# Cosformer attention with a mixture of adapters: v issued earlier, the adapter transpose copied by VectorE, and a new order in a few places

## The chip, the cores and the metric

The kernel runs on one core of one Trainium2 chip. The metric is the device time of one execution in microseconds (us); lower is better. Five engines work side by side, each through its own queue in program order: TensorE (PE in the profile, its weight loads PEld), VectorE (DVE), ScalarE (ACT), GpSimd (POOL) and SyncE (SP), which here only issues transfers. Transfers (DMAs) are issued from SP, from POOL and, at the very end, from ACT.

## What is computed

Two steps, cut to what matters. Inputs q, k, v are 8 batches x 8 heads x 576 positions x 64 floats; the output is 4608 x 512 floats.

```
phi(x) = concat(relu(x) * cos_w, relu(x) * sin_w)      # per position, 64 -> 128 features
kv  = einsum('bhsf,bhsd->bhfd', phi(k), v)             # 128 x 64 per batch and head
z   = sum over s of phi(k)
num = phi(q) @ kv ;  den = phi(q) @ z + 1e-6
x   = (num / den), heads side by side: 4608 rows x 512

logits = x @ w_gate                                    # 8 adapters
topk = the two largest; w = softmax over the two
out = x + sum over the two of w * ((x @ A[e]) @ B[e])  # rank 16 adapters
```

## The kernel before

**Tiles and slots.** The 4608 rows are 36 tiles of 128 rows (NT = 36). A tile has two "columns" of 64 rows (a batch and a residue of its positions modulo 9), so 9 tiles make a pair of batches. The main loop (L433) has one step per tile, called slot n below. A slot holds the work of several tiles in different stages: tile n is normalised, the numerators and denominators of tile n+1 are computed, the scaled q of tile n+2 is transposed, q of tile n+3 is scaled. The order is written out by hand: the helpers are called in the order in which each engine shall get its instructions, and the tiles' semaphores make an engine wait at the head of its queue until the operands are there.

**Attention.** `scale_k(u)` makes phi(k) of one of 72 units (batch b, residue i; u = 9b + i) with two ScalarE instructions (L159, L170). `kv(u)` (L187) adds 8 small matmuls into the PSUM tile `kvz`; after the ninth unit of a batch `kv_out` (L192) copies it to SBUF. The table `kv_at` says in which slot which units are multiplied; their `scale_k` stands one slot ahead. `scale_q` (L205) makes phi(q) without the relu on GpSimd, `transp_q` (L215) transposes it on TensorE, `evac_q` (L220) applies the relu and copies it out on VectorE, `numden` (L229, L234) multiplies with kv, and `normalise` (L241, L243) divides.

**Adapters.** `transp_x` (L250) and `evac_x` (L255) bring x of tile n to the other layout in the PSUM tile `xz` (columns 0 to 511), `logits` (L276) multiplies by A and w_gate. Tiles form groups of three (the last two groups have two and one). For a group whose last tile is t, slot t+1 ("age 1") has `gate_max` (three small VectorE operations and two on GpSimd, nm L296 and tg L298). Slot t+2 ("age 2") has the sigmoid `gate_sig` (L306, ScalarE), the masking `gate_em` (L313, GpSimd), `gate_b` (L340, VectorE) and `transp_z` (L348), which transposes zg into columns 512 to 895 of the same `xz`. Slot t+3 ("age 3") begins with `evac_z` (L356), which copies this to `zgT` on ScalarE. From there on one `delta` per slot adds x (L366) and the adapters' share (L367) in the single PSUM tile `dx`; `evac_o` (L375, ScalarE) copies it out and `store` (L387) issues two transfers from SP. Ages 1, 2 and 3 follow each other, so every slot from 3 on is one of the three kinds; the age 3 slots are 5, 8, 11 and so on to 32, and tile 35 is handled behind the loop.

**Loads.** k and q come as fp32 from SP (1152 KB per batch; four buffers each, the first v sharing those of k). v of batches 1 to 7 is cast to bf16 by transfers that GpSimd issues (L83; four buffers); v of batch 0 comes as fp32 and is cast on the engines (L413 to L416). The tables at L400 and L401 say at the end of which slot a load is called: k and q of batches 4 to 7 in slots 1, 5, 10 and 14, v of batches 2 to 7 in slots 3, 6, 9, 13, 17 and 21. v of batch 1 is called before the loop (L421), behind the scaling of tile 0. A load stands in its issuing engine's queue like any other instruction: an SP load is behind the stores called before it, a GpSimd load is behind the `scale_q` and gate operations called before it.

**Buffers that matter.** `qp` has 3, `kp` 10, `osb` (what is stored) 14; `xz`, `dx`, `kvz`, `nd` and the transposed q have one PSUM tile each.

**The end.** Behind the loop (L486 to L522) tile 35 and the last six deltas are written out one by one; the za, nd and dx tiles serve as accumulators there.

Of the kernel before, what the change touches and what calls it, by code (L numbers as in the profile page):

```python
# [25 lines left out]
def kernel(ctx, tc, q, k, v, w_gate, A, Bw, out):  # L26
    nc = tc.nc
# [53 lines left out]
    def load_v(b):  # L81
        t = v_bufs[b % NV][:, 0:VL].rearrange("p (j x) -> p j x", j=HP)
        nc.gpsimd.dma_start(out=t, in_=part(v, b))  # L83
# [113 lines left out]
        cols = [(2 * m, i) for i in range(NC)] + [(2 * m + 1, i) for i in range(NC)]  # L197
        return cols[2 * s:2 * s + 2]

    def scale_q(n, x, eng=None):  # L200
        if x == 0:
            qp_t[n] = p_qp.tile([128, 2, HP, 2, D], BF16, name="qp")
        b, i = columns(n)[x]
        for t, tab in ((0, cos_tab), (1, sin_tab)):
            (eng or nc.gpsimd).tensor_scalar(out=qp_t[n][:, x, :, t, :], in0=q_t[b][:, :, i, :],  # L205
                                             scalar1=tab[:, i:i + 1], scalar2=1.0,
                                             op0=ALU.mult, op1=ALU.mult)

# [14 lines left out]
    def numden(n):  # L223
        nd_t[n] = nd = ps.tile([128, 2, 512], FP32, name="nd")
        qpT = qpT_t.pop(n)
        (b0, _), (b1, _) = columns(n)
        jobs = [(slice(0, 128), b0)] if b0 == b1 else [(lo, b0), (hi, b1)]
        for gg in range(2):
            nc.tensor.matmul(out=nd[:, gg, D:4 * W:W], lhsT=ones, rhs=eps_hi, start=True,  # L229
                             stop=False, skip_group_check=True)  # L230
            for jj in range(4):
                h = gg * 4 + jj
                for pr, b in jobs:
                    nc.tensor.matmul(out=nd[pr, gg, jj * W:(jj + 1) * W], lhsT=qpT[:, h, pr],  # L234
                                     rhs=kv_t[b][:, h % 2, h // 2, :],
                                     start=False, stop=(jj == 3), skip_group_check=True)
# [13 lines left out]
            nc.tensor.transpose(out=xz[:, c * 128:(c + 1) * 128],  # L250
                                in_=xt_t[n][:, c:DM:DCH], identity=ident)

    def evac_x(n):
        xT_t[n] = t = p_xt.tile([128, DCH, 128], BF16, name="xT")
        nc.vector.tensor_copy(t, xz[:, 0:512].rearrange("p (c s) -> p c s", c=DCH))  # L255

    groups = [list(range(i, min(i + 3, NT - 3))) for i in range(0, NT - 3, 3)]
    groups += [[NT - 3, NT - 2], [NT - 1]]
# [89 lines left out]
            nc.tensor.transpose(out=xz[:, 512 + i * 128:512 + (i + 1) * 128], in_=zg[:, i],  # L348
                                identity=ident)

    def evac_z(g, on_act=False):
        G = len(groups[g])
        zgT_t[g] = t = p_g.tile([128, 3, 128], BF16, name="zgT")
        src = xz[:, 512:512 + G * 128].rearrange("p (c s) -> p c s", c=G)
        if on_act:
            nc.scalar.copy(t[:, 0:G], src)  # L356
        else:
            nc.vector.tensor_copy(t[:, 0:G], src)

    def delta(n, bank=None):  # L360
        g = group_of[n]
        if bank is None:
            dx = ps.tile([128, DM], FP32, name="dx", tag="dx")
        else:
            dx = bank
        nc.tensor.matmul(out=dx, lhsT=ident, rhs=xt_t.pop(n), start=True, stop=False)  # L366
        nc.tensor.matmul(out=dx, lhsT=zgT_t[g][:, n - groups[g][0], :], rhs=Ball,  # L367
                         start=False, stop=True)
        osb_t[n] = dx

    def evac_o(n, how="act"):
        src = osb_t[n]
# [22 lines left out]
    for b in range(4, B):  # L395
        n0 = NS * (b // 2) - 6 if b % 2 == 0 else NS * (b // 2) - 1
        for n, cnt in enumerate((2, 2, 2, 2, 1) if b % 2 == 0 else (3, 2, 2, 2)):
            kv_at[n0 + n] = range(u, u + cnt)
            u += cnt
    kq_at = {1: 4, 5: 5, 10: 6, 14: 7}  # L400
    v_at = {3: 2, 6: 3, 9: 4, 13: 5, 17: 6, 21: 7}  # L401

    warm_ps = ps.tile([128, DM], FP32, name="warm_ps", tag="dx")

# [7 lines left out]
    v0b = v_bufs[0][:, 0:VL].rearrange("p (j i d) -> p j i d", j=HP, i=NC)  # L412
    nc.vector.tensor_copy(v0b[:, :, 0:4, :], v0[:, :, 0:4, :])  # L413
    nc.gpsimd.tensor_copy(v0b[:, :, 4, :], v0[:, :, 4, :])
    nc.vector.tensor_copy(v0b[:, 0:3, 5:NC, :], v0[:, 0:3, 5:NC, :])
    nc.gpsimd.tensor_copy(v0b[:, 3, 5:NC, :], v0[:, 3, 5:NC, :])  # L416
    for u in range(NC):
        kv(u)
    scale_q(0, 0)
    scale_q(0, 1, nc.vector)  # L420
    load_v(1)  # L421
    transp_q(0)
    evac_q(0)
    kv_out(0)
    for n in (1, 2):
        scale_q(n, 0)
        scale_q(n, 1)
    transp_q(1)
    numden(0)
    fill(5)  # L430

    todo = []
    for n in range(NT - 1):  # L433
        age = {n - t[-1]: g for g, t in enumerate(groups)}
        if n + 3 < NT:
            scale_q(n + 3, 0)
        normalise(n)
        if 2 in age:
            gate_sig(age[2])
            gate_em(age[2])  # L440
        if 3 in age:
            evac_z(age[3], True)
            todo += groups[age[3]]
        if n >= 2:
            for u in kv_at.get(n + 1, ()):
                scale_k(u)
        if n == 3:
            nc.vector.tensor_copy(AW[:, :, 0:ER].rearrange("p c (e r) -> p e c r", e=E), AWf)
            nc.vector.tensor_copy(AW[:, :, ER:ZW], Gf)
            nc.vector.tensor_copy(Ball, Bf)  # L450
        if n + 3 < NT:
            scale_q(n + 3, 1)
        transp_x(n)
        for t in due.get(n, ()):
            logits(t)
        evac_q(n + 1)
        numden(n + 1)
        evac_x(n)
        if n < 2:
            for u in kv_at.get(n + 1, ()):  # L460
                scale_k(u)
        if n + 2 < NT:
            transp_q(n + 2)
        if 1 in age:
            gate_max(age[1])
        if 2 in age:
            gate_b(age[2])
        for u in kv_at.get(n, ()):
            kv(u)
            if u % NC == NC - 1:  # L470
                kv_out(u // NC)
        for d in todo[:1]:
            delta(d)
            evac_o(d)
            store(d)
        del todo[:1]
        if 2 in age:
            transp_z(age[2])
        if n in v_at:
            load_v(v_at[n])  # L480
        if n in kq_at:
            load_k(kq_at[n])
            load_q(kq_at[n])


    n = NT - 1  # L486
    ga, gb, gc = len(groups) - 3, len(groups) - 2, len(groups) - 1
    assert not todo and groups[ga:] == [[n - 5, n - 4, n - 3], [n - 2, n - 1], [n]]
    normalise(n)
    evac_z(ga, True)  # L490
    logits(n - 1)
    transp_x(n)
    gate_max(gb)
    gate_sig(gb)
    gate_em(gb)
    delta(n - 5)
    evac_x(n)
    za_bank = ps.tile([128, DM], FP32, name="dx_za", tag="za")
    delta(n - 4, za_bank)
    logits(n)  # L500
    evac_o(n - 5)
    evac_o(n - 4)
    gate_b(gb)
    gate_last(gc)
    transp_z(gb)
    delta(n - 3)
    gate_last_em(gc)
    gate_b(gc)
    evac_z(gb)
    transp_z(gc)  # L510
    nd_banks = ps.tile([128, 2, DM], FP32, name="dx_nd", tag="nd")
    delta(n - 2, nd_banks[:, 0])
    delta(n - 1, nd_banks[:, 1])
    evac_z(gc)
    evac_o(n - 3)
    evac_o(n - 2)
    evac_o(n - 1, "dve")
    za_bank = ps.tile([128, DM], FP32, name="dx_za", tag="za")
    delta(n, za_bank)
    evac_o(n, "both")  # L520
    for d in range(n - 5, n + 1):
        store(d, nc.gpsimd if d < n - 1 else nc.scalar)  # L522
# [30 lines left out]
```

## Time and profile before

| what | value |
|---|---|
| median of 3 runs | 146.74 us (145.67 to 149.4) |
| the profiled execution's own time | 146.11 us |
| its span, first to last instruction | 144.3 us |
| busy: PE, DVE, ACT, POOL | 106.6, 88.6, 86.4, 82.9 us |
| mean granted TensorE clock | 0.927 |
| DMA packets moved | 34.44 MB (v counted after its cast) |
| read from and written to HBM | 28.85 MB, 9.44 MB |

So 1.8 us of the profiled execution lie outside its span. In the lines of the profile, "[0.89 <-ACT zgT L356]" is idle time of the engine just before an instruction and the instruction that ended it; "x24" means 24 instructions merged into one line. "PEclk" is the clock granted to TensorE as a share of its full clock. In the rows by stage, "DMA share" is the mean busy share of the 16 DMA engines; it can be over 1 where packets of two queues overlap.

### The profile page before, as it was taken

The page shows a single profiled execution, that of the slowest core. Times are in us where ns is not written, and L with a number is a line of the kernel's source. Part 1 is how long each engine was busy: PE and PEld are TensorE (multiplying, and loading weights), DVE is VectorE, ACT ScalarE, POOL GpSimd, SP SyncE. Part 2 cuts the span into 40 slices and gives each one's busy share as a digit, 9 for nine tenths or more (in the row PEclk, how much of TensorE's full clock was granted, in tenths as well). Part 3 has the DMA queues.
Part 4 walks back from the last instruction along what each step waited for, and adds up shares of the span by engine and source line. Part 5 has one row for each costly group of instructions (what it writes and reads, how often), then busy time and mean ns, then how long its engine had stood idle before and what let it go on. Part 6 is the DMA issues. An engine that isn't in the chain of part 4 may idle for free.

```text
span 144.3 us, 4295 instructions
## 1 busy us (share of the span) xinstructions
PE 106.6 (74%) x1682; PEld 80.1 (55%) x1682; DVE 88.6 (61%) x252; ACT 86.4 (60%) x205; POOL 82.9 (57%) x199
## 2 busy tenths in 40 slices
PE   4994755987309975779979589797994979888630
PEld 1353445866207863557856377675864758575310
DVE  3554573786402569065779658696783877979630
ACT  7641970059103689097894969979679693324620
POOL 2047398559300796184597865959688285831520
PEclk9999985697775899599999999999999999999999
DMA  4999999999993899996999999948853253543884
GB/s 98 374 355 383 360 243 355 394 388 365 290 359 130 203 289 310 354 191 136 408 348 237 265 324 308 272 125 111 238 117 81 58 122 77 118 100 81 183 245 149
DMA packets 21236, 34.44 MB, mean 239 GB/s; under 512 B 2784, under 2 KB 9440, under 8 KB 21216
## 3 DMA queue, kind: packets, MB, share of 16 engines
q1 hardware_dynamic: 17168, 29.25, 63.2%
q0 software_dynamic: 3888, 4.65, 18.8%
q8 instruction: 13, 0.21, 0.6%
q10 hardware_dynamic: 160, 0.26, 0.5%
q14 instruction: 7, 0.06, 0.1%
HBM read 28.85 MB, written 9.44 MB: 265 GB/s over the span
## 4 chain that ended last, share of the span: by engine, by line
PE 39%; DMA 32%; ACT 11%; DVE 7%; issue 4%; SPq 1%; POOL 1%; DVEq 1%; ACTq 0%; POOLq 0%
DMA v<-in_v_dram 24%; PE kvz L187 10%; PE qpTp L215 6%; DMA qs<-in_q_dram 6%; PE xz L250 5%; PE za L276 5%; PE nd L234 5%; PE dx L366 5%; PE dx L367 3%; ACT zgT L356 3%; ACT osb L375 2%; DVE xt L243 2%; ACT kp L170 2%; ACT kp L159 2%; DMA out_dram<-osb 2%
## 5 line engine op out<-in xcount | busy, mean ns | idle before, releaser
L159 ACT ACTIVATE kp<-ks,cos_tab 128x256 bf16<-128x256 f32 x72 | 35.1, 501 | 2.9 <-DMA ks<-in_k_dram 2.9
L205 POOL TENSOR_SCALAR qp<-qs,cos_tab 128x256 bf16<-128x256 f32 x71 | 33.9, 477 | 4.0 <-PE xz L250 2.3
L375 ACT COPY osb<-dx 128x512 f32<-128x512 f32 x32 | 18.7, 583 | 29.0 <-PE dx L367 28.6
L205 POOL TENSOR_SCALAR qp<-qs,sin_tab 128x256 bf16<-128x256 f32 x71 | 33.7, 475 | 0.0
L255 DVE COPY xT<-xz 128x512 bf16<-128x512 bf16 x36 | 15.2, 423 | 29.5 <-PE xz L250 29.5
L170 ACT ACTIVATE kp<-ks,sin_tab 128x256 bf16<-128x256 f32 x61 | 30.4, 498 | 0.0
L187 PE MATMUL kvz<-v,kp 64*128 64x128 bf16 x576 | 23.1, 231 | 9.8 <-DMA v<-in_v_dram 9.8
L215 PE MATMUL qpTp<-ident,qp 128*128 128x128 bf16 x288 | 24.1, 230 | 3.5 <-POOL qp L205 3.5
L187 PEld LDWEIGHTS <-kp 64*128 64x128 bf16 x576 | 18.5, 101 | 13.2 <-issue 10.9
L243 DVE TENSOR_TENSOR xt<-nd,rden 128x512 bf16<-128x512 f32 x36 | 24.9, 691 | 1.2
L220 DVE TENSOR_SCALAR qpT<-qpTp 128x1024 bf16<-128x1024 bf16 x36 | 24.5, 681 | 1.4 <-PE qpTp L215 1.4
L250 PE MATMUL xz<-ident,xt 128*128 128x128 bf16 x144 | 15.1, 231 | 13.5 <-ACT zgT L356 12.3
L250 PEld LDWEIGHTS <-xt 128*128 128x128 bf16 x144 | 11.7, 118 | 21.7 <-issue 10.4
L215 PEld LDWEIGHTS <-qp 128*128 128x128 bf16 x288 | 18.1, 103 | 4.4 <-POOL qp L205 4.3
L296 POOL TENSOR_TENSOR nm<-m 128x3 f32<-128x3 f32 (+1 forms) x12 | 2.3, 194 | 31.0 <-DVE m L290 31.0
L234 PE MATMUL nd<-kvsb,qpT 128*128 128x65 bf16 (+1 forms) x320 | 17.3, 200 | 1.8 <-DVE qpT L220 1.8
L234 PEld LDWEIGHTS <-qpT 128*128 128x128 bf16 (+1 forms) x320 | 13.0, 103 | 3.3 <-DVE qpT L220 2.8
L192 ACT CAST kvsb<-kvz 128x520 bf16<-128x520 f32 x8 | 4.7, 588 | 16.0 <-PE kvz L187 16.0
L276 PE MATMUL za<-AW,xT 128*128 128x136 bf16 x144 | 13.2, 231 | 0.0
L366 PE MATMUL dx<-xt,ident 128*128 128x512 bf16 x32 | 12.8, 401 | 0.0
L367 PE MATMUL dx<-Ball,zgT 128*128 128x512 bf16 x32 | 12.6, 395 | 0.0
L229 PE MATMUL nd<-eps_hi,ones 128*128 128x4 bf16 x72 | 12.1, 174 | 0.0
(66 smaller groups left out, 108.9 us busy)
## 6 DMA issues: line engine op xcount, KB each, us to landing
out_dram<-osb SPq DMA_DIRECT2D x66, 128.0 KB, 3.2
ks<-in_k_dram SPq DMA_DIRECT2D x7, 1152.0 KB, 8.4
qs<-in_q_dram SPq DMA_DIRECT2D x7, 1152.0 KB, 12.3
v<-in_v_dram POOLq DMA_DIRECT2D x7, 576.0 KB, 11.1
ks<-in_k_dram SPq DMA_DIRECT2D x1, 640.0 KB, 4.3
ks<-in_v_dram SPq DMA_DIRECT2D x1, 640.0 KB, 6.5
qs<-in_q_dram SPq DMA_DIRECT2D x1, 640.0 KB, 12.4
ks<-in_k_dram SPq DMA_DIRECT2D x1, 512.0 KB, 5.3
```

The lines of the kernel that those rows point to most:

```text
L159: nc.scalar.activation(kp[:, :, 0, :], src, AF.Relu, bias=0.0, scale=cos_tab[:, i:i + 1])
L170: nc.scalar.activation(kp[:, :, 1, :], src, AF.Relu, bias=0.0, scale=sin_tab[:, i:i + 1])
L187: nc.tensor.matmul(out=kvz_t[b][:, a, j], lhsT=kp[pr, j], rhs=v_rhs(b, j, i, pr), start=(i == 0 and j == 0), stop=(i == NC - 1 and j == HP ...
L205: (eng or nc.gpsimd).tensor_scalar(out=qp_t[n][:, x, :, t, :], in0=q_t[b][:, :, i, :], scalar1=tab[:, i:i + 1], scalar2=1.0, op0=ALU.mult, ...
L215: nc.tensor.transpose(out=t[:, j, :, x, :], in_=qp[:, x, j], identity=ident)
L220: nc.vector.tensor_scalar(out=t, in0=src.rearrange("p j a x s -> p (j a) (x s)"), scalar1=0.0, scalar2=None, op0=ALU.max)
L234: nc.tensor.matmul(out=nd[pr, gg, jj * W:(jj + 1) * W], lhsT=qpT[:, h, pr], rhs=kv_t[b][:, h % 2, h // 2, :], start=False, stop=(jj == 3), ...
L243: nc.vector.tensor_tensor(out=xt, in0=nd[:, :, :, 0:D], in1=rden.rearrange("p (g j) -> p g j", g=2).to_broadcast([128, 2, 4, D]), op=ALU.mult)
L250: nc.tensor.transpose(out=xz[:, c * 128:(c + 1) * 128], in_=xt_t[n][:, c:DM:DCH], identity=ident)
L276: nc.tensor.matmul(out=za_t[g][:, i, :], lhsT=xT[:, c, :], rhs=AW[:, c, :], start=(c == 0 and i == 0), stop=(c == DCH - 1), skip_group_che ...
L366: nc.tensor.matmul(out=dx, lhsT=ident, rhs=xt_t.pop(n), start=True, stop=False)
L375: nc.scalar.copy(t, src)
```

## The change

- **v and the other loads.** The call of v of batch 1 moves ahead of the second half of the casts of v of batch 0. v of batches 2 to 7 is called in slots 0, 3, 7, 11, 15 and 19. k of batches 5, 6 and 7 is called in slots 4, 7 and 11, q of batch 5 in slot 4; the others stay.
- **zgT.** `evac_z` is always on VectorE and is called behind `evac_x`, `gate_max` and `gate_b` of its slot instead of at its head.
- **Gate.** `gate_sig` moves from the head of the age 2 slot to the end of the age 1 slot, ahead of that slot's `evac_o`; `gate_em` becomes the first call of the age 2 slot, ahead of `scale_q`.
- **The start.** `scale_q(0, 0)` is split between GpSimd and ScalarE. `numden(0)` and the filling matmuls stand ahead of `transp_q(1)` on TensorE; there are 4 instead of 5 of these, and 3, 2 and 1 more in slots 0, 1 and 2.
- **The end.** `delta` is split into `delta_x` and `delta_b`, which may be called apart. `logits(34)` moves into slot 34, the gate operations of the group of tiles 33 and 34 stand ahead of `normalise(35)`, `evac_x(35)` is on ScalarE, and the last deltas, gates and copies have a new order.

```diff
--- before.py
+++ after.py
@@ -197,14 +197,17 @@
         cols = [(2 * m, i) for i in range(NC)] + [(2 * m + 1, i) for i in range(NC)]
         return cols[2 * s:2 * s + 2]
 
-    def scale_q(n, x, eng=None):
+    def scale_q(n, x, engs=None):
         if x == 0:
             qp_t[n] = p_qp.tile([128, 2, HP, 2, D], BF16, name="qp")
         b, i = columns(n)[x]
-        for t, tab in ((0, cos_tab), (1, sin_tab)):
-            (eng or nc.gpsimd).tensor_scalar(out=qp_t[n][:, x, :, t, :], in0=q_t[b][:, :, i, :],
-                                             scalar1=tab[:, i:i + 1], scalar2=1.0,
-                                             op0=ALU.mult, op1=ALU.mult)
+        for t, (tab, eng) in enumerate(zip((cos_tab, sin_tab), engs or (nc.gpsimd,) * 2)):
+            to, src, by = qp_t[n][:, x, :, t, :], q_t[b][:, :, i, :], tab[:, i:i + 1]
+            if eng is nc.scalar:
+                eng.activation(to, src, AF.Relu, bias=0.0, scale=by)
+            else:
+                eng.tensor_scalar(out=to, in0=src, scalar1=by, scalar2=1.0, op0=ALU.mult,
+                                  op1=ALU.mult)
 
     def transp_q(n):
 
@@ -250,9 +253,13 @@
             nc.tensor.transpose(out=xz[:, c * 128:(c + 1) * 128],
                                 in_=xt_t[n][:, c:DM:DCH], identity=ident)
 
-    def evac_x(n):
+    def evac_x(n, on_act=False):
         xT_t[n] = t = p_xt.tile([128, DCH, 128], BF16, name="xT")
-        nc.vector.tensor_copy(t, xz[:, 0:512].rearrange("p (c s) -> p c s", c=DCH))
+        src = xz[:, 0:512].rearrange("p (c s) -> p c s", c=DCH)
+        if on_act:
+            nc.scalar.copy(t, src)
+        else:
+            nc.vector.tensor_copy(t, src)
 
     groups = [list(range(i, min(i + 3, NT - 3))) for i in range(0, NT - 3, 3)]
     groups += [[NT - 3, NT - 2], [NT - 1]]
@@ -348,25 +355,22 @@
             nc.tensor.transpose(out=xz[:, 512 + i * 128:512 + (i + 1) * 128], in_=zg[:, i],
                                 identity=ident)
 
-    def evac_z(g, on_act=False):
+    def evac_z(g):
         G = len(groups[g])
         zgT_t[g] = t = p_g.tile([128, 3, 128], BF16, name="zgT")
-        src = xz[:, 512:512 + G * 128].rearrange("p (c s) -> p c s", c=G)
-        if on_act:
-            nc.scalar.copy(t[:, 0:G], src)
-        else:
-            nc.vector.tensor_copy(t[:, 0:G], src)
-
-    def delta(n, bank=None):
+        nc.vector.tensor_copy(t[:, 0:G], xz[:, 512:512 + G * 128].rearrange(
+            "p (c s) -> p c s", c=G))
+
+    def delta_x(n, bank=None):
+        if bank is None:
+            bank = ps.tile([128, DM], FP32, name="dx", tag="dx")
+        nc.tensor.matmul(out=bank, lhsT=ident, rhs=xt_t.pop(n), start=True, stop=False)
+        osb_t[n] = bank
+
+    def delta_b(n):
         g = group_of[n]
-        if bank is None:
-            dx = ps.tile([128, DM], FP32, name="dx", tag="dx")
-        else:
-            dx = bank
-        nc.tensor.matmul(out=dx, lhsT=ident, rhs=xt_t.pop(n), start=True, stop=False)
-        nc.tensor.matmul(out=dx, lhsT=zgT_t[g][:, n - groups[g][0], :], rhs=Ball,
+        nc.tensor.matmul(out=osb_t[n], lhsT=zgT_t[g][:, n - groups[g][0], :], rhs=Ball,
                          start=False, stop=True)
-        osb_t[n] = dx
 
     def evac_o(n, how="act"):
         src = osb_t[n]
@@ -397,8 +401,9 @@
         for n, cnt in enumerate((2, 2, 2, 2, 1) if b % 2 == 0 else (3, 2, 2, 2)):
             kv_at[n0 + n] = range(u, u + cnt)
             u += cnt
-    kq_at = {1: 4, 5: 5, 10: 6, 14: 7}
-    v_at = {3: 2, 6: 3, 9: 4, 13: 5, 17: 6, 21: 7}
+    k_at = {1: 4, 4: 5, 7: 6, 11: 7}
+    q_at = {1: 4, 4: 5, 10: 6, 14: 7}
+    v_at = {0: 2, 3: 3, 7: 4, 11: 5, 15: 6, 19: 7}
 
     warm_ps = ps.tile([128, DM], FP32, name="warm_ps", tag="dx")
 
@@ -412,35 +417,31 @@
     v0b = v_bufs[0][:, 0:VL].rearrange("p (j i d) -> p j i d", j=HP, i=NC)
     nc.vector.tensor_copy(v0b[:, :, 0:4, :], v0[:, :, 0:4, :])
     nc.gpsimd.tensor_copy(v0b[:, :, 4, :], v0[:, :, 4, :])
+    load_v(1)
     nc.vector.tensor_copy(v0b[:, 0:3, 5:NC, :], v0[:, 0:3, 5:NC, :])
     nc.gpsimd.tensor_copy(v0b[:, 3, 5:NC, :], v0[:, 3, 5:NC, :])
     for u in range(NC):
         kv(u)
-    scale_q(0, 0)
-    scale_q(0, 1, nc.vector)
-    load_v(1)
+    scale_q(0, 0, (nc.gpsimd, nc.scalar))
+    scale_q(0, 1, (nc.vector, nc.vector))
     transp_q(0)
     evac_q(0)
     kv_out(0)
     for n in (1, 2):
         scale_q(n, 0)
         scale_q(n, 1)
+    numden(0)
+    fill(4)
     transp_q(1)
-    numden(0)
-    fill(5)
 
     todo = []
     for n in range(NT - 1):
         age = {n - t[-1]: g for g, t in enumerate(groups)}
+        if 2 in age:
+            gate_em(age[2])
         if n + 3 < NT:
             scale_q(n + 3, 0)
         normalise(n)
-        if 2 in age:
-            gate_sig(age[2])
-            gate_em(age[2])
-        if 3 in age:
-            evac_z(age[3], True)
-            todo += groups[age[3]]
         if n >= 2:
             for u in kv_at.get(n + 1, ()):
                 scale_k(u)
@@ -465,12 +466,22 @@
             gate_max(age[1])
         if 2 in age:
             gate_b(age[2])
+        if 3 in age:
+            evac_z(age[3])
+            todo += groups[age[3]]
+        if n < 3:
+            fill(3 - n)
+        if n == NT - 2:
+            logits(n)
         for u in kv_at.get(n, ()):
             kv(u)
             if u % NC == NC - 1:
                 kv_out(u // NC)
+        if 1 in age:
+            gate_sig(age[1])
         for d in todo[:1]:
-            delta(d)
+            delta_x(d)
+            delta_b(d)
             evac_o(d)
             store(d)
         del todo[:1]
@@ -478,45 +489,51 @@
             transp_z(age[2])
         if n in v_at:
             load_v(v_at[n])
-        if n in kq_at:
-            load_k(kq_at[n])
-            load_q(kq_at[n])
+        if n in k_at:
+            load_k(k_at[n])
+        if n in q_at:
+            load_q(q_at[n])
 
 
     n = NT - 1
     ga, gb, gc = len(groups) - 3, len(groups) - 2, len(groups) - 1
     assert not todo and groups[ga:] == [[n - 5, n - 4, n - 3], [n - 2, n - 1], [n]]
-    normalise(n)
-    evac_z(ga, True)
-    logits(n - 1)
-    transp_x(n)
     gate_max(gb)
     gate_sig(gb)
     gate_em(gb)
-    delta(n - 5)
-    evac_x(n)
+    normalise(n)
+    delta_x(n - 5)
     za_bank = ps.tile([128, DM], FP32, name="dx_za", tag="za")
-    delta(n - 4, za_bank)
+    delta_x(n - 4, za_bank)
+    transp_x(n)
+    evac_z(ga)
+    evac_x(n, True)
+    gate_b(gb)
+    delta_b(n - 5)
+    delta_b(n - 4)
+    nd_banks = ps.tile([128, 2, DM], FP32, name="dx_nd", tag="nd")
+    delta_x(n - 3, nd_banks[:, 0])
+    transp_z(gb)
     logits(n)
+    evac_z(gb)
     evac_o(n - 5)
     evac_o(n - 4)
-    gate_b(gb)
     gate_last(gc)
-    transp_z(gb)
-    delta(n - 3)
+    delta_b(n - 3)
+    delta_x(n - 2, nd_banks[:, 1])
+    delta_b(n - 2)
     gate_last_em(gc)
     gate_b(gc)
-    evac_z(gb)
     transp_z(gc)
-    nd_banks = ps.tile([128, 2, DM], FP32, name="dx_nd", tag="nd")
-    delta(n - 2, nd_banks[:, 0])
-    delta(n - 1, nd_banks[:, 1])
+    za_bank = ps.tile([128, DM], FP32, name="dx_za", tag="za")
+    delta_x(n, za_bank)
+    delta_x(n - 1)
     evac_z(gc)
+    delta_b(n - 1)
+    delta_b(n)
     evac_o(n - 3)
     evac_o(n - 2)
     evac_o(n - 1, "dve")
-    za_bank = ps.tile([128, DM], FP32, name="dx_za", tag="za")
-    delta(n, za_bank)
     evac_o(n, "both")
     for d in range(n - 5, n + 1):
         store(d, nc.gpsimd if d < n - 1 else nc.scalar)
```

## Prediction

> **What bounds the kernel now.** I read the chain of work that ended last first, then the list of waits.
>
> ```profile
> 12.55 11.14 DMA v<-in_v_dram
> 23.74 1.89 PE kvz L187 x32
> ...
> 30.84 12.13 DMA v<-in_v_dram
> 43.01 1.46 PE kvz L187 x24
> ...
> 47.29 11.39 DMA v<-in_v_dram
> 58.73 1.46 PE kvz L187 x24
> ```
> ```profile
> PE xz L250 <- ACT zgT L356: 12.3, 11, 2.2
> PE kvz L187 <- DMA v<-in_v_dram: 9.8, 3, 5.8
> DVE zg L340 <- POOL em L313: 3.7, 10, 0.5
> ```
>
> Three loads of v lie on the chain, each from its issue on GpSimd to its landing. TensorE is in order, so a `kv` without its v (1.48, 5.78 and 2.53 us) stops everything behind it: transposes, normalisation, and GpSimd's next scaling. Behind 65 us v is gone from the chain; the gaps in TensorE's work there end with ScalarE's zgT copy. The slot lines show why:
>
> ```profile
> 81.56 0.11 PEld L250 LDWEIGHTS <-xt 128*128 128x128 bf16 x1 [0.37 <-DVE xt L243]
> ...
> 82.06 0.57 ACT L192 CAST kvsb<-kvz 128x520 bf16<-128x520 f32 x1
> ...
> 82.53 0.58 ACT L375 COPY osb<-dx 128x512 f32<-128x512 f32 x1
> ...
> 83.00 0.48 ACT L356 COPY zgT<-xz 128x384 bf16<-128x384 bf16 x1
> ...
> 83.54 0.39 PE L250 MATMUL xz<-ident,xt 128*128 128x128 bf16 x4 [2.17 <-ACT zgT L356]
> ```
>
> x of the tile was ready at 81.56. The copy stood behind scale_k, kvsb and osb in ScalarE's queue, and the next transposes write the same tile `xz`. The stages show the other limits (columns: span, busy us of PE, PEld, DVE, ACT, POOL, PEclk, DMA share, GB/s):
>
> ```profile
> 23.70:26.90 3.20, 3.16 (x51) 2.96 (x51) 0.61 (x2) 0.00 (x0) 3.20 (x8) 0.50 1.06 390
> ...
> 43.00:47.30 4.30, 4.29 (x51) 3.54 (x51) 1.30 (x8) 1.82 (x5) 0.37 (x3) 0.50 0.36 141
> 47.30:58.70 11.40, 7.86 (x139) 6.19 (x137) 7.65 (x20) 8.63 (x21) 8.62 (x20) 0.95 1.03 287
> 58.70:66.40 7.70, 6.40 (x104) 5.11 (x104) 2.84 (x7) 5.20 (x14) 4.41 (x11) 0.80 0.89 222
> 66.40:92.40 26.00, 21.57 (x402) 16.89 (x400) 19.25 (x53) 20.93 (x51) 18.29 (x44) 1.00 1.04 299
> ```
>
> After a wait for v TensorE runs at 0.50 clock. And the DMA engines are full up to 92 us except at 43 to 47 us, when everything asked for had come: v2 was late because it was asked for late.
>
> **The change part by part** (against the span of 144.3 us; minus is a gain).
>
> *v, -9.8.* In the GpSimd line, `scale_q` of tile 3 ends at 21.3 us; v2, now behind it, is issued there instead of at 30.84. v1 goes out at 9.3 (end of the cast L414) instead of 12.55. Each issue costs GpSimd 0.82 to 0.98 us as before; only its place moves. v3 (slot 3 instead of 6) stands where v2 stood. All three waits go, as far as the last term doesn't bring them back.
>
> *Clock, -4.5.* TensorE's busy time at half clock behind the three waits is 3.2 + 4.3 + 3.1 us (58.7 to 61.8, where 24 matmuls take 1.46 us and 0.84 elsewhere). Half of it is 5.2; the other end is 0, if VectorE set the pace there. In the lines TensorE runs without gaps, so I stay near 5.2.
>
> *zgT, -9.5, and +1.0.* Of the 12.3 us, TensorE would have stood for x anyway in a part: x was ready 0.65 of 1.01 us ahead at 74, 1.9 of 2.17 at 83.5, 0.85 of 0.89 at 92, 0.5 of 0.89 at 126.8. Read off so, 2.2 us of the first three waits (2.7) and 7.3 of the other eight (9.5) count. Ends: 6 and 12.3. VectorE gets 11 copies; by its rows for 256 (278 ns) and 512 (423 ns) columns 384 take 0.35 us, in all 3.9. They follow `evac_x`, where VectorE waits for `nd` in age 3 slots (0.27 us at 75.2), and tile n+1's x is needed 1.3 us later. Ends 0 and 3.9, I take 1.0. The first `delta_b` now waits for VectorE, but kv and `delta_x` (0.5 + 0.3 us) stand ahead of it.
>
> *Sigmoid, -1.0.* The mask reaches VectorE without the 0.4 us that zg waits in most age 2 slots, so normalise follows sooner; TensorE stood for x only in some (0.50 at 73.4). Ends 0 and 3.7. The sigmoid now holds `evac_o` until GpSimd's tg; at 87.8 to 88.0 tg is done 0.7 us before `dx` (88.75), so nothing is late behind it. On GpSimd `gate_em` now leads `scale_q`, which works three tiles ahead.
>
> *Start, +1.0 and +0.3.* A k or q load takes 2.9 us alone (k2 lands at 28.6, q2 at 31.5, each issue plus its time to landing) and 4.4 beside v (k3 34.5, q3 39.2, k4 43.4). v1, 3.2 us sooner, so takes a third of the rate from the second part of q0 (issued at 5.15, 12.4 us to landing), for which GpSimd's next scaling starts only at 17.68: +1.0 (0 to 1.6). The cast L416 comes 0.4 us later, the split of tile 0's scaling saves 0.5, `numden(0)` no longer waits for tile 1's q (15.7 to 14.1): all hidden by that wait for q0, price 0; without it they are worth 0.5 at most. Five more filling matmuls (1.24 us for five) stand mostly in gaps: +0.3 (0 to 1.2).
>
> *SP.* k5, k6, k7 pass the stores of one or three slots. Their buffers are free by then; q5 waits a slot for tile 8's scaling and holds a few stores. Stores come some 3 us later; 14 buffers cover it, price 0. Without the cover ScalarE would stop in `evac_o`.
>
> *New waits, +3.5.* v2 to v7 now follow each other on one queue. At the 11.4 to 12.1 us each took beside other loads, v2 lands at 22.3 + 11.7 = 34.0, v3 at 45.4, v4 at 56.8 (53.9 if it takes 8.5 as at 56.4). TensorE asked for them at 37.2, 56.1 and 69.7 (waits included); with the gains up to there (2.4, 11 and 15.9: the v waits, clock and zgT waits that lie before, less the 1.3 of the start) at 34.8, 45.1 and 53.8. So: 0.3, 0.3, then up to 3.0; I take 2.0, and 0.9 for v6 and k. k2 lands at 31 instead of 28.6, 3 us before its first product. Ends: 0, and 9, if each v takes 12.1 and k follows.
>
> *End, -1.0.* Behind the last zgT copy six 512-column matmuls (137.38 to 138.40) become two: -0.6. TensorE's 0.55 us wait for zgT at 133.8 goes, VectorE takes the copy and ScalarE `evac_x`. Ends +0.5 and -2.
>
> Sum: -9.8 - 4.5 - 9.5 + 1.0 - 1.0 + 1.0 + 0.3 + 3.5 - 1.0 = -20.0, span 124.3. The profiled execution is 1.8 longer than its span, and the median 0.6 above it: **126.7 us**.
>
> *A page against the rows.* By the rows, v takes a third of the rate from the other queue, 390 to 400 GB/s alone. The Trainium skill, "DMA: Bandwidth & Descriptors", section "Issuing engines are not separate DMA queues", says that all issuers share the same 16 engines: an earlier issue adds no rate, and what v gains k and q lose. The full DMA share up to 43 us agrees. Its section "Queues, rings and completion order" has the engines take turns by packet between queues; by that v would get half, land in some 6 us (an estimate from this page), and the new waits would be some 1.5 instead of 3.5: 124.7. The measured 11 to 12 us per v decide.
>
> **The rivals.**
> *1. DMA becomes the bound (130 to 134).* A k or q costs 2.95 us of the engines, a v 4.0 (12.1 us beside it hold 2.75 loads instead of 4.1), a tile's store 0.75 (what is left of 47.3 to 92.4 after six k or q and four v, over 15 tiles). Ahead of v7: 17 times 2.95, 7 times 4.0, 22 stores, the weights 1.4, from 2.2 us on: 98. TensorE asked for v7 at 111.9; less the 17.3 of the sum's terms that lie before, the forecast asks at 94.6. From there to the end were 32.4 us, 29.5 without the last zgT waits and the end's 1.0. So 98 + 29.5, 1.5 to 4 for half clock after new waits, and 2.4 outside: 131 to 134; 130 if stores give way. For it: the DMA share near 1. Against: stores can lag by 14 tiles.
> *2. The zgT gain is given back (136 to 138).* In an age 3 slot something else ends as late: ScalarE (2.3 us a slot) or VectorE. Without the -9.5 and -1.0: 137.2. Against: x was ready early at 83.5, and ScalarE loses work.
> *3. Slower: GpSimd is held at the issue of a v behind an unfinished one.* SP shows that an issue can be held: 9.64 us for the 16 KB of the gates at 9.74. At 8.8 us for each of six issues, less the 3 us that `scale_q` is ahead, 35 us: 161. It decides from 3.9 us net per issue (23.5 us, slower by over 2%). Against: the issue at 56.4 took 0.82 us with v3 still under way until 58.7.
> *4. v lands no sooner* because only the place in the program moves: 144 to 148 with rival 2. Against: GpSimd reached the new place at 21.3.
>
> **How the numbers follow.** Forecast 0.68 (its own range 121.5 to 131: about half of the terms' ends at once), rival 1 0.17, rival 2 0.07, rival 3 0.04, rival 4 0.04. 121.5 to 136 leaves out half of rival 2, rivals 3 and 4 and a little below. 2% is about what a measurement of this kernel can tell from no change. Faster: 0.68 + 0.17 + 0.07 = 0.92; same 0.04 (rival 4); slower 0.04 (rival 3).
>
> **What would show it.** Right: v2 issued near 22 us and landed by 35; TensorE's waits for v under 4 us in all; no wait of L250 for zgT; PEclk near 1 from 25 us on; tile 14 normalised near 58 instead of 72.4; age 3 slots as long as the others. Wrong: waits of ScalarE or GpSimd for k or q beyond 3 us (rival 1), L250 or L366 waiting for something else in age 3 slots (2), long L83 issues (3).

## The result, and the profile after

The changed kernel takes 123.7 us (median of 4 runs, 123.51 to 124.3), the kernel before in the same place 146.2 us (4 runs, 144.46 to 149.4). The ratio is 0.853, with a 95% interval of 0.846 to 0.861. Some executions of a kernel take over 1.5% longer than the quickest of the same kernel; the ratios here and below leave those out, the medians and the stated ranges do not. The profiled execution took 123.69 us, its span is 121.9 us and its mean granted clock 0.958. Against the profiled execution of before the span is 22.4 us shorter; the prediction had 20.0, and a time of 126.7 us.

Chain of work of the changed kernel, first 60 us (columns: start, duration, what):

```profile
3.11 8.46 DMA qs<-in_q_dram
11.76 2.46 POOL qp L209 x5
14.21 5.62 issue
20.79 0.94 POOL qp L209 x2
...
22.38 1.28 PE warm_ps L412 x3
...
36.48 0.78 PE kvz L187 x24
```

None of the three loads of v is left on the chain. A `kv` of 24 matmuls takes 0.78 us instead of 1.46, which is the full clock. What stands at the front now is q of batch 0. The chain calls 14.21 to 19.83 "issue", but GpSimd's line shows that it is a load:

```profile
19.88 0.48 POOL L209 TENSOR_SCALAR qp<-qs,cos_tab 128x256 bf16<-128x256 f32 x1 [5.66 <-DMA qs<-in_q_dram]
...
23.48 0.82 POOL L83 DMA_DIRECT2D v<-in_v_dram  x1
...
32.02 0.81 POOL L83 DMA_DIRECT2D v<-in_v_dram  x1
...
43.01 0.82 POOL L83 DMA_DIRECT2D v<-in_v_dram  x1
```

v2, v3 and v4 are issued at 23.48, 32.02 and 43.01 and land at 35.6, 43.9 and 54.8. The list of waits, with the groups that were read before and those that replace them:

```profile
POOL qp L209 <- DMA qs<-in_q_dram: 6.5, 2, 5.7
...
PE xz L253 <- DVE xt L246: 2.1, 7, 0.5
...
DVE zg L347 <- POOL em L320: 0.9, 2, 0.6
...
PE nd L237 <- ACT kvsb L192: 1.0, 2, 0.5
```

The 12.3 us of `xz` behind zgT and the 9.8 us of `kvz` behind v have no line any more, and VectorE's 3.7 us behind the mask are 0.9. The stages (columns as in the prediction):

```profile
23.70:30.80 7.10, 7.10 (x136) 5.75 (x134) 5.02 (x12) 0.59 (x1) 6.23 (x13) 0.82 1.09 351
30.80:43.00 12.20, 11.03 (x217) 8.88 (x215) 11.02 (x34) 9.37 (x24) 9.26 (x23) 1.00 1.10 317
...
69.00:92.00 23.00, 22.15 (x415) 17.51 (x414) 20.25 (x58) 20.98 (x51) 19.39 (x47) 1.00 0.98 299
```

From 30.8 us to 108 us the clock is 1.00. In these two later stretches TensorE is busy for 90 and 96%, VectorE for 90 and 88%, ScalarE for 77 and 91%: no engine stands out any more.

**Where the 22.4 us came from.** Each tile's normalisation starts with one small reciprocal on VectorE (L241, now L244), so its start times are a ruler through both traces. Tiles 4 and 14, before and after:

```profile
30.51 0.21 DVE L241 RECIPROCAL rden<-nd 128x8 f32<-128x8 f32 x1
...
72.38 0.20 DVE L241 RECIPROCAL rden<-nd 128x8 f32<-128x8 f32 x1
...
31.63 0.20 DVE L244 RECIPROCAL rden<-nd 128x8 f32<-128x8 f32 x1
...
57.56 0.20 DVE L244 RECIPROCAL rden<-nd 128x8 f32<-128x8 f32 x1
```

| from | before | after | difference |
|---|---|---|---|
| start to tile 4 | 30.5 | 31.6 | +1.1 |
| tile 4 to tile 14 | 41.9 | 26.0 | -15.9 |
| tile 14 to tile 35 | 60.1 | 52.7 | -7.4 |
| tile 35 to the end | 11.8 | 11.6 | -0.2 |

Sorted by the kind of slot, the stretch behind tile 14 says more. The seven age 3 slots from 14 to 32 took 22.8 us in all and take 17.5; the six age 2 slots from 16 to 31 took 16.5 and take 13.9; the seven age 1 slots did not change (18.6 and 18.6). Slot 34, which leads to tile 35, is 0.6 us longer.

### The profile page after: what moved, and what is told of

The parts are those of the page before. It is cut to its first block, busy times and chain, and to the rows that moved or that the text cites. A ratio compares the mean times of both kernels' runs of the same rounds, so it can differ in the third digit from the quotient of the medians.

```text
span 121.9 us, 4288 instructions
## 1 busy us (share of the span) xinstructions
PE 101.3 (83%) x1687; PEld 75.1 (62%) x1687; DVE 90.5 (74%) x262; ACT 82.8 (68%) x196; POOL 82.2 (67%) x198
## 3 DMA queue, kind: packets, MB, share of 16 engines
q0 software_dynamic: 3888, 4.65, 21.2%
## 4 chain that ended last, share of the span: by engine, by line
PE 42%; DVE 17%; ACT 15%; DMA 9%; issue 8%; POOL 3%; SPq 2%; ACTq 0%; POOLq 0%
PE kvz L187 9%; PE qpTp L218 8%; DMA qs<-in_q_dram 7%; PE nd L237 6%; ACT kp L170 6%; ACT kp L159 5%; DVE xt L246 5%; PE dx L367 5%; PE xz L253 4%; PE za L283 4%; POOL qp L209 3%; PE dx L372 3%; DVE qpT L223 3%; DVE xT L262 2%; ACT osb L379 2%
## 5 line engine op out<-in xcount | busy, mean ns | idle before, releaser
L218 PE MATMUL qpTp<-ident,qp 128*128 128x128 bf16 x288 | 23.0, 224 | 4.7 <-POOL qp L209 4.7
L379 ACT COPY osb<-dx 128x512 f32<-128x512 f32 x31 | 18.1, 583 | 9.1 <-PE dx L372 9.1
L187 PE MATMUL kvz<-v,kp 64*128 64x128 bf16 x576 | 21.0, 217 | 0.5 <-DVE v L421 0.4
L218 PEld LDWEIGHTS <-qp 128*128 128x128 bf16 x288 | 17.3, 100 | 5.7 <-POOL qp L209 5.3
L237 PE MATMUL nd<-kvsb,qpT 128*128 128x65 bf16 (+1 forms) x320 | 16.8, 196 | 3.5 <-DVE qpT L223 2.4
L187 PEld LDWEIGHTS <-kp 64*128 64x128 bf16 x576 | 16.3, 94 | 4.7 <-issue 1.8
L253 PEld LDWEIGHTS <-xt 128*128 128x128 bf16 x144 | 10.7, 116 | 9.8 <-DVE xt L246 6.4
L253 PE MATMUL xz<-ident,xt 128*128 128x128 bf16 x144 | 14.6, 225 | 2.2 <-DVE xt L246 2.1
L283 PE MATMUL za<-AW,xT 128*128 128x136 bf16 x144 | 12.5, 223 | 0.0
L232 PE MATMUL nd<-eps_hi,ones 128*128 128x4 bf16 x72 | 11.9, 170 | 0.0
L412 PE MATMUL warm_ps<-idle 128*128 128x512 bf16 x34 | 11.2, 484 | 0.0
## 6 DMA issues: line engine op xcount, KB each, us to landing
v<-in_v_dram POOLq DMA_DIRECT2D x7, 576.0 KB, 11.6
qs<-in_q_dram SPq DMA_DIRECT2D x1, 640.0 KB, 14.4
```

Source lines behind the costliest of these rows:

```text
L187: nc.tensor.matmul(out=kvz_t[b][:, a, j], lhsT=kp[pr, j], rhs=v_rhs(b, j, i, pr), start=(i == 0 and j == 0), stop=(i == NC - 1 and j == HP ...
L253: nc.tensor.transpose(out=xz[:, c * 128:(c + 1) * 128], in_=xt_t[n][:, c:DM:DCH], identity=ident)
L283: nc.tensor.matmul(out=za_t[g][:, i, :], lhsT=xT[:, c, :], rhs=AW[:, c, :], start=(c == 0 and i == 0), stop=(c == DCH - 1), skip_group_che ...
L379: nc.scalar.copy(t, src)
```

## The experiments

The theory to be tested is the prediction's: earlier issue removes the waits for v and the half clock behind them, zgT on VectorE removes the wait for `xz`, and the two add up. The rivals: the transfers are the bound, the zgT gain is given back, or the small parts (sigmoid, fillers, end) carry a share that the prediction put elsewhere. In batches of runs on other chips the kernel before had medians of 145.98 to 148.06, so times are compared within 1 us only where their runs don't overlap. "T4", "T14" and "T35" below are the starts of the normalisation of these tiles.

**The loads alone** (before, with the new places of k, q and v):

```diff
-    kq_at = {1: 4, 5: 5, 10: 6, 14: 7}
-    v_at = {3: 2, 6: 3, 9: 4, 13: 5, 17: 6, 21: 7}
+    k_at = {1: 4, 4: 5, 7: 6, 11: 7}
+    q_at = {1: 4, 4: 5, 10: 6, 14: 7}
+    v_at = {0: 2, 3: 3, 7: 4, 11: 5, 15: 6, 19: 7}
...
     nc.gpsimd.tensor_copy(v0b[:, :, 4, :], v0[:, :, 4, :])
+    load_v(1)
```

> The kernel before with the new load tables and the new place of v of batch 1 alone. Theory 1 (the waits for v with their half clock are one loss, the zgT waits another): TensorE waits for v under 1 us; tile 14 is normalised at 60 (72.4 less 9.8 and 4.5, plus 2 for the later q0); the waits of L250 for zgT stay at 10 to 13 us; span 144.3 - 12.3 = 132, time 134. Rival (the fillers and the rest are needed to use the early v; without them half clock or zgT waits take the place): 138 or more, PEclk at 0.5 to 0.7 in slices between 30 and 65 us.

Measured: 136.65 us (134.43 to 137.51; no interval could be given), span 135.7. The profiled execution is the longest of the four, 3 us longer than the shortest, which is the one near the expected 134. In it T4 to T14 fell from 41.9 to 30.6 us; tile 14 came at 62.2 instead of the expected 60. The waits for v are gone, and those for zgT stay as they were:

```profile
PE xz L250 <- ACT zgT L356: 11.8, 10, 2.2
```

**All but the loads** (the changed kernel with the old tables and the old place of v1):

```diff
-    k_at = {1: 4, 4: 5, 7: 6, 11: 7}
-    q_at = {1: 4, 4: 5, 10: 6, 14: 7}
-    v_at = {0: 2, 3: 3, 7: 4, 11: 5, 15: 6, 19: 7}
+    kq_at = {1: 4, 5: 5, 10: 6, 14: 7}
+    v_at = {3: 2, 6: 3, 9: 4, 13: 5, 17: 6, 21: 7}
...
-    load_v(1)
...
     scale_q(0, 1, (nc.vector, nc.vector))
+    load_v(1)
```

> The changed kernel with the loads' old tables and the old place of v of batch 1. Theory 1: the waits for v come back at 9 to 12 us, zgT waits stay away; the gain is that of zgT, gate and end, 8 to 10, so 136 to 138. Rival (zgT's waits only hid behind the wait for v, or the new order needs the early v): 142 or more. Other rival (the loads matter little, the fillers keep the clock): 130 or less.

Measured: 137.37 us, ratio 0.948 (0.934 to 0.962), span 136.6. The waits for v did not stay at 9.8 us; they grew:

```profile
PE kvz L187 <- DMA v<-in_v_dram: 15.2, 4, 7.5
```

Behind tile 14, where no v is late, this kernel is as quick as the changed one (53.6 against 52.7 us). Between T4 and T14 it takes 40.6 us, hardly less than before. Faster slots reach the next `kv` sooner, and v2 and v3, issued at the same slots, are as late as ever in time (31.05 and 47.34 us, before 30.84 and 47.29).

**zgT alone** (before, with the copy on VectorE behind `gate_b`):

```diff
-        if 3 in age:
-            evac_z(age[3], True)
-            todo += groups[age[3]]
...
         if 2 in age:
             gate_b(age[2])
+        if 3 in age:
+            evac_z(age[3])
+            todo += groups[age[3]]
```

> The kernel before with nothing but the zgT copy on VectorE at the end of its slot in the loop (the one behind the loop stays on ScalarE). Theory 1: the waits of L250 for zgT go (12.3 to under 1 us), the five steps of slots 14 to 29 that held them shorten by 0.7 to 1.9 us each, 7 us in all and 1 us of it given back by VectorE: 138 to 140. Rival (in age 3 slots something else ends as late, the sigmoid being still late): 143 or more.

Measured: 137.73 us, ratio 0.947 (0.930 to 0.965). The age 3 slots from 14 to 32 fell from 22.8 to 16.1 us and the other slots behind tile 14 stayed, so the gain is real and is not given back there. Between T4 and T14 nothing was won (41.7 against 41.9 us), for the same reason as above:

```profile
PE kvz L187 <- DMA v<-in_v_dram: 12.3, 3, 6.9
...
PE xz L250 <- ACT zgT L356: 0.6, 1, 0.6
```

Of the 12.3 us of waits for zgT, 0.6 are left.

The two halves are therefore more than additive in the stretch where v is late: T4 to T14 shrinks by 11.3 us with the loads alone, by 1.2 with all the rest alone, and by 15.9 with both.

**v1 late again** (changed kernel):

```diff
-    load_v(1)
...
     scale_q(0, 1, (nc.vector, nc.vector))
+    load_v(1)
```

> The changed kernel with v of batch 1 issued at its old place behind the scaling of tile 0; v of batches 2 to 7 stays early. Theory 2 (v of batch 1 takes its rate from the second part of q0, which then holds the start): the second part of q0 lands at 17.6 instead of 19.9, tile 2 is normalised near 22.5 instead of 24.6, and the time falls by 1.5 to 2.2 to 122. Rival (the transfers up to 55 us are the bound, so what the start gains is lost again in a wait for v2 or v4): 123.7 within 0.5, with TensorE waiting 1 to 2 us for v.

Measured: 121.33 us (121.03 to 122.63), ratio 0.836 (0.823 to 0.849). The runs lie below all of the changed kernel's; the intervals of the two ratios still overlap a little. In the profiled execution T14 is at 56.4 instead of 57.6. GpSimd's and TensorE's lines show both sides of the trade:

```profile
17.42 0.48 POOL L209 TENSOR_SCALAR qp<-qs,cos_tab 128x256 bf16<-128x256 f32 x1 [2.20 <-DMA qs<-in_q_dram]
...
23.46 1.89 PE L187 MATMUL kvz<-v,kp 64*128 64x128 bf16 x32 [0.60 <-DMA v<-in_v_dram]
```

The second part of q0 lands 2.5 us sooner, so T2 is at 21.2 instead of 24.6. Then `kv` waits 0.60 us for v1 and runs at half clock, which takes back two thirds of it (T4 30.5 against 31.6). So v1 was worth less at its new place than the q0 that it delayed.

**q0 ahead of k1 on SP** (changed kernel), and the same with q of batches 4 to 7 later:

```diff
     load(q_t[0], q, 0, 0, 4)
-    load_k(1)
     load(q_t[0], q, 0, 4, NC)
+    load_k(1)
...
-    q_at = {1: 4, 4: 5, 10: 6, 14: 7}
+    q_at = {6: 4, 8: 5, 12: 6, 15: 7}
```

The first block alone:

> The changed kernel (v of batch 1 early) with the second part of q0 issued on SP ahead of k of batch 1. Theory 2 (the start is held by the second part of q0 alone): it lands near 15 instead of 19.9, k of batch 1 near 18, tile 3 is normalised at 24 to 25 instead of 28.0, and the gain of 3 to 4 stays to the end: 120 to 121. Rival (up to 55 us the transfers are the bound): GpSimd issues v2 earlier, but v2, k2 or v4 land no more than 1 us earlier, TensorE waits 2 to 3 us for v2 or v4: 122.5 to 123.7.

Both blocks:

> As e5_q0_first, with q of batches 4 to 7 called in slots 6, 8, 12 and 15 instead of 1, 4, 10 and 14: fewer loads stand beside v3, v4 and k3. If the transfers are the bound in slots 3 to 12, this gives another 1 to 2 us against e5_q0_first; if not, the same within 0.4, or a wait of GpSimd for q.

Measured: 122.29 us (121.72 to 122.61) and 122.08 us (121.91 to 123.75). The first is faster than the changed kernel; the second can't be told from the first. T2 is at 21.9 and 21.1, but now k1 is late, and by T4 (30.5 and 29.8) the first stands where the late v1 stood. ScalarE's wait of the first:

```profile
ACT kp L159 <- DMA ks<-in_k_dram: 7.5, 2, 5.8
```

The first missed its forecast of 120 to 121: tile 3 came at 25.7, not at 24 to 25. So up to 30 us three loads (k1, v1 and the second part of q0) compete, and each of the orders tried only chose which of them is late. That looks like a bound by transfers, but of the start alone: behind it neither these two kernels nor the changed one wait for a v, k or q, and a later q bought nothing that could be measured.

**Without the fillers of slots 0 to 2** (changed kernel):

```diff
-        if n < 3:
-            fill(3 - n)
```

> The changed kernel without the 3, 2 and 1 filling matmuls of slots 0 to 2 (the 4 ahead of transp_q(1) stay). Theory (they stand on TensorE's path at half clock, 1.28 us at 22.4 and 0.85 at 25.4 in the chain, and don't lift the clock in time): 122.3 to 123.3, clock 0.5 to 0.7 from 20 to 30 us. Rival (they are what brings the full clock by 26 us, where the kv of batch 1 take 1.08 us instead of 1.89): 124.5 or more.

Measured: 124.03 us (123.78 to 125.49), not to be told from the changed kernel. The fillers stand on the chain (1.28 us at 22.38), but without them T4 is at 31.8 instead of 31.6: they neither cost nor gain here that could be measured.

**The old end** (changed kernel with the last block of before, and `logits(34)` back in it):

```diff
+    normalise(n)
+    evac_z(ga, True)
+    logits(n - 1)
+    transp_x(n)
     gate_max(gb)
     gate_sig(gb)
     gate_em(gb)
-    normalise(n)
-    delta_x(n - 5)
...
```

> The changed kernel with the end behind the loop as it was before (and logits of tile 34 behind the loop again). The prediction's step (the new end is worth 1.0): 124.7. Rival from the trace of after (from tile 34's normalisation to the end it takes 14.4 us, before 14.0): 123.3 to 123.7, not slower.

Measured: 123.24 us (6 runs, 122.86 to 123.4), 0.5 below the changed kernel; the runs of the two don't overlap. In the profiled executions tile 34 to the end takes 14.1 instead of 14.4 us. The new end is no gain but a small loss. Two places show it: `gate_max` now stands on VectorE ahead of `normalise(35)`, so the step from tile 34 to tile 35 takes 2.82 us instead of 2.24, and ScalarE's copy of x of tile 35 waits for the copy of zgT on the changed kernel's VectorE, which reads the same tile `xz`:

```profile
112.15 0.59 ACT L260 COPY xT<-xz 128x512 bf16<-128x512 bf16 x1 [1.17 <-DVE zgT L361]
```

**The old place of the gate** (changed kernel):

```diff
-        if 2 in age:
-            gate_em(age[2])
...
         normalise(n)
+        if 2 in age:
+            gate_sig(age[2])
+            gate_em(age[2])
...
-        if 1 in age:
-            gate_sig(age[1])
```

> The changed kernel with the sigmoid and gate_em at their old places in the age 2 slot. The prediction's step (the early sigmoid is worth 1.0): 124.7, with VectorE waiting 2 to 4 us for em at zg. Rival (worth nothing, since TensorE is held by something else in age 2 slots): 123.5 to 123.9.

Measured: 126.39 us (125.88 to 126.91), 2.7 slower than the changed kernel. Slot 16 of this kernel shows the path, sigmoid on ScalarE, mask on GpSimd, then VectorE waiting for it ahead of the next tile:

```profile
65.37 0.23 ACT L313 ACTIVATE u<-tg 128x24 f32<-128x24 f32 x1
...
65.90 0.23 POOL L320 TENSOR_TENSOR em<-u,mask 128x24 f32<-128x24 f32 x1
...
66.16 0.56 DVE L347 TENSOR_TENSOR zg<-za,em 128x384 bf16<-128x384 f32 x1 [0.61 <-POOL em L320]
...
66.63 0.20 DVE L244 RECIPROCAL rden<-nd 128x8 f32<-128x8 f32 x1
```

The age 2 slots from 16 to 31 take 16.8 us with the old gate and 13.9 with the new one, but the age 3 slots from 14 to 32 go the other way, 15.9 to 17.5. There something else is late next. The changed kernel's slot 17:

```profile
64.79 0.40 PE L187 MATMUL kvz<-v,kp 64*128 64x128 bf16 x8
...
66.07 0.50 ACT L170 ACTIVATE kp<-ks,sin_tab 128x256 bf16<-128x256 f32 x1
...
66.47 0.57 ACT L192 CAST kvsb<-kvz 128x520 bf16<-128x520 f32 x1
...
67.10 0.28 PE L237 MATMUL nd<-kvsb,qpT 128*128 128x65 bf16 x4 [0.50 <-ACT kvsb L192]
...
67.57 0.21 DVE L244 RECIPROCAL rden<-nd 128x8 f32<-128x8 f32 x1 [0.72 <-PE nd L237]
```

The last `kv` of the batch is done at 65.2, but kvsb stands behind `scale_k` in ScalarE's queue until 66.47, and the next numerators wait 0.50 us for it. TensorE reached them sooner than ScalarE could.

**v1 late, old end and later q together** (changed kernel; the end is edited as in the kernel with the old end):

```diff
-    q_at = {1: 4, 4: 5, 10: 6, 14: 7}
+    q_at = {6: 4, 8: 5, 12: 6, 15: 7}
...
-    load_v(1)
...
     scale_q(0, 1, (nc.vector, nc.vector))
+    load_v(1)
...
+    normalise(n)
+    evac_z(ga, True)
+    logits(n - 1)
+    transp_x(n)
     gate_max(gb)
...
```

> The changed kernel with v of batch 1 at its old place, the old end, and q of batches 4 to 7 called in slots 6, 8, 12 and 15. If the gains of e4_v1_late (2.4) and e8_old_end (0.4) add up: 120.5 to 121. If the transfers of slots 1 to 3 held e4's start, the late q4 gives another 0.5: 120 to 120.5. Otherwise as e4_v1_late, 121.3.

Measured: 121.53 us (120.77 to 122.22), ratio 0.843 (0.834 to 0.851). It beats the changed kernel, but not the late v1 alone (121.33). The three small changes did not add up to anything that could be measured, and the later q now costs GpSimd two waits of 0.24 and 1.06 us.

**Before, with the clock kept up** (filling matmuls ahead of three `kv`):

```diff
+    warm_at = {1: 5, 5: 16, 10: 9}
...
+        if n in warm_at:
+            fill(warm_at[n])
         for u in kv_at.get(n, ()):
```

> The kernel before with 5, 16 and 9 filling matmuls (as long as the waits for v or shorter) ahead of the kv that wait in slots 1, 5 and 10. They do no useful work; only the clock behind the waits changes. The prediction's step (half clock behind the waits is worth 4.5): tile 14 is normalised at 68 to 69.5 instead of 72.4, PEclk 0.9 or more from 43 to 47 us. Rival (what TensorE loses at half clock hides behind VectorE, GpSimd and the next wait for v, which comes from the transfers): 71.5 to 72.4, the waits for v longer by what the clock gave.

Measured: 147.44 us (146.88 to 148.23), ratio 1.020 (1.012 to 1.029). As a whole it failed, because the third set was put in the wrong slot: the third wait for v is in slot 9, and the nine fillers of slot 10 ran on the path. The first two sets did their work. T4 came at 28.9 instead of 30.5, and T7, behind the second, at 44.5 instead of 46.9:

```profile
41.33 0.85 PE L187 MATMUL kvz<-v,kp 64*128 64x128 bf16 x24 [3.41 <-DMA v<-in_v_dram]
...
56.60 1.47 PE L187 MATMUL kvz<-v,kp 64*128 64x128 bf16 x24 [2.81 <-DMA v<-in_v_dram]
...
60.59 3.15 PE L408 MATMUL warm_ps<-idle 128*128 128x512 bf16 x9
```

With fillers ahead the `kv` behind its wait takes 0.85 us, without them 1.47. So the half clock alone, with v called in the same slots as ever, is worth 2.4 us at the first two places (1.6 by T4, 0.8 more by T7); the prediction's sum has 3.2 for these two. The third was not measured, and T14 came at 73.3, outside both ranges that were expected.

**v4 to v7 one slot later** (changed kernel):

```diff
-    v_at = {0: 2, 3: 3, 7: 4, 11: 5, 15: 6, 19: 7}
+    v_at = {0: 2, 3: 3, 8: 4, 12: 5, 16: 6, 20: 7}
```

> The changed kernel with v of batches 4 to 7 called one slot later (8, 12, 16, 20). Theory (v lands 11 to 12 us behind its issue whatever else happens, and v4 had 0.5 us in hand: 43.0 + 11.8 = 54.8 against 55.3): v4 issued near 45.8 lands near 57.3, TensorE waits 1.8 to 2.5 us in slot 12 and not for v5 to v7 (4 us and more in hand): 125.5 to 126.5. Rival (the amount of transfers ahead sets the landing, not the issue): v4 lands by 55.8 and the time stays within 0.5 of 123.7.

Measured: 125.15 us (124.83 to 127.24), 1.45 slower than the changed kernel. GpSimd's issue of v4, and TensorE's `kv` that needs it:

```profile
44.86 0.82 POOL L83 DMA_DIRECT2D v<-in_v_dram  x1
...
56.88 0.62 PE L187 MATMUL kvz<-v,kp 64*128 64x128 bf16 x16 [1.44 <-DMA v<-in_v_dram]
```

Issued 1.85 us later than in the changed kernel, v4 lands 12.0 us after its issue, and TensorE waits 1.44 us, a little less than the 1.8 to 2.5 that were expected. The step from tile 13 to 14 is 1.5 us longer and everything behind it is unchanged. v5, v6 and v7, 2.5 to 3.9 us later, cost nothing. This tells the place of issue from the rate of the transfers as the cause: the bytes, and the order within each queue, are the same.

## Why the prediction was right, and where it was not

Each row puts the prediction's terms beside what was measured. Spans of profiled executions are used, as the prediction's sum did. The wait of v1 and the half clock behind it belong to the start; the 4.5 us of clock are divided over the three stretches as their half clock times (3.2, 4.3, 3.1).

| step | forecast | measured | from |
|---|---|---|---|
| start, to tile 4 | -1.6 (-1.5 - 1.4 + 1.0 + 0.3) | +1.1 | T4, changed kernel against before |
| waits for v2, v3 and their half clock | -11.4 (-8.3 - 3.1) | -11.3 | T4 to T14, loads alone |
| zgT | -8.5 (-9.5 + 1.0) | -9.7 | age 3 slots, see below |
| sigmoid | -1.0 | -2.5 | span, old gate against changed |
| new waits | +3.5 | 0 | no wait for v or, behind the start, for k or q |
| end | -1.0 | +0.4 | tile 34 to the end, 14.0 and 14.4 |
| sum | -20.0 | -22.0 | the span: -22.4 |

0.4 us are not assigned to a step. That the sum came within 2.4 us of the span is in part luck: the start and the end missed by 2.7 and 1.4 us in one direction, the new waits, the sigmoid and zgT by 3.5, 1.5 and 1.2 us in the other.

**Waits for v and half clock: right.** v2 was issued at 23.48 (forecast near 22) and landed at 35.6 (by 35). The mechanism, an issue called at too late a slot, is shown from both sides: the loads alone take the waits away, loads put back bring 15.2 us of them, and one slot is enough to bring one back. How much of the 11.3 is half clock is less well known: the fillers ahead of `kv` won 2.4 us at the first two places, the sum had 3.2 there. The clock was to be near 1 from 25 us on; it was so from 27 us on.

**zgT: right, in mechanism and size.** 6.7 us of it come from the slots 14 to 32 (zgT alone), 3.0 from the slots 5, 8 and 11 (9.6 us in the loads-alone kernel, 6.6 with the old gate). Reading each wait off against the moment when x was ready gave 9.5 where the plain sum of the list would have given 12.3. The predicted sign, age 3 slots as long as the others, is there: 2.5 us on average behind tile 14, against 2.3 for age 2 and 2.7 for age 1. The lines of slot 17 show what ends last in that slot now, kvsb.

**Start: wrong, by 2.7 us.** The step that failed is "v1, 3.2 us sooner, so takes a third of the rate from the second part of q0: +1.0 (0 to 1.6)". It came 2.2 us later (19.88 instead of 17.68), TensorE stood 4 us for the scaled q, its clock fell, and the gain on v1's wait was used up. The late v1 brought 1.1 us back in the profiled execution and 2.4 in the medians.

**New waits: wrong, 3.5 that did not come.** The step "v2 to v7 now follow each other on one queue" put v3 at 45.4 and v4 at 56.8. They landed at 43.9 and 54.8, each 11.9 and 11.8 us after its own issue, although v3 was issued while v2 was still under way for 3.6 us. TensorE asked at 46.4 and 55.3:

```profile
46.37 0.84 PE L187 MATMUL kvz<-v,kp 64*128 64x128 bf16 x24
...
55.33 0.62 PE L187 MATMUL kvz<-v,kp 64*128 64x128 bf16 x16
```

So nothing was late, but for v4 the margin was 0.5 us, and the run with these loads one slot later shows what the forecast had feared. The first 0.3 of the term does not follow from its own figures either: v2 at 34.0 is ahead of the asking at 34.8.

**Sigmoid: right in sign, too small.** The prediction counted only the slots in which TensorE was seen to wait for x. Against the old gate all six age 2 slots from 16 to 31 are shorter, by 0.2 to 0.7 us each, 2.9 in all; slot 16 shows how, VectorE's wait for the mask delays its next normalisation. What came back in age 3, 1.6 us behind tile 14, is in the -2.5, which lies within the stated end of -3.7.

**End: wrong in sign, small.** Four matmuls less behind the last copy were counted; the three gate operations that VectorE gets ahead of `normalise(35)`, and ScalarE's wait for VectorE's copy, were not.

**Rivals.** The transfers were not the bound (rival 1): its sum had the stores of 22 tiles ahead of v7, and SP had issued those of nine when v7 was called at 73.7. The stores gave way, and no engine of the changed kernel waited for them. Rival 2 is refuted by zgT alone, rival 3 by the issues of v, of which those at 32.02 and 43.01 took 0.81 and 0.82 us with another v under way, and rival 4 by the landings.

## What to carry to other kernels

A load can be late by its place in the issuing queue alone, even with a DMA share near 1. Then place it by the time of its first use less the measured time from issue to landing, and recompute the place after every other speed-up, because faster slots ask sooner. Price a wait in a list by what would have been late next, not by its length, and sort the slots by kind to see where a gain lands and where a part of it comes back. At the start of this kernel, moving one load ahead moved another back; look in such a place at which one the first stalled engine needs.

## What the runs showed of the hardware

**In the changed kernel a v load took nearly the same time wherever it was issued.** All seven, the group of L83 on GpSimd:

```profile
L83 POOL DMA_DIRECT2D v<-in_v_dram x7: 810/817/950, 9.5 to 73.7; - x7
...
DMA to landing us min/median/max: 10.9/11.6/12.1
```

That holds for v2 at 23.48, beside SP's long k and q loads, and for v6 at 62.83, beside stores and q (10.9 us). It does not hold for every kernel here: 8.8 us for the v issued at 18.14 with q0 ahead of k1, and 8.5, 8.0 and 6.8 us for those at 56.43, 72.72 and 96.47 in the kernel before. What made these quicker was not tested.

**SP's issues were held at times, GpSimd's were not.** In the changed kernel SP's issue of the 16 KB of the gates took 9.85 us, of two k loads 5.40 and 9.34 us, while each v was issued in 0.81 to 0.95 us.

**The clock fell without a long pause.** In the kernel with v1 late TensorE's longest pause ahead of the fall was 1.51 us (to 18.41). The stages of one microsecond (columns as before):

```profile
17.00:18.00 1.00, 0.00 (x0) 0.00 (x0) 0.96 (x4) 1.00 (x4) 0.58 (x2) 1.00 1.13 300
18.00:19.00 1.00, 0.40 (x4) 0.23 (x4) 0.36 (x1) 1.00 (x3) 1.00 (x3) 1.00 1.11 289
19.00:20.00 1.00, 0.68 (x7) 0.44 (x8) 0.24 (x1) 1.00 (x4) 1.00 (x3) 1.00 1.15 271
20.00:21.00 1.00, 1.00 (x17) 0.87 (x16) 0.82 (x2) 1.00 (x3) 1.00 (x3) 0.74 1.19 211
21.00:22.00 1.00, 1.00 (x11) 0.95 (x10) 0.83 (x3) 0.13 (x1) 0.95 (x3) 0.50 1.19 221
```

TensorE was busy for 1.08 of the 3 us from 17 to 20, and the clock was at 0.50 from 21 us on. The Trainium skill, "TensorE: Matmul & The Clock Gate", section "What's actually happening", gives an idle window of some 3.4 us as the condition. Here 3 us that were busy for a third were enough, and no pause of that length was needed. A threshold on activity would fit these rows. So would a count that leaves out transposes, which were TensorE's only work from 16.9 to 19.56. No run here tells the two apart or shows where a threshold lies.
